# Norm steps and weight combinations moved in the last two matrix products of a fused attention, mixture and relu-squared kernel

## Chip, cores and metric

One core of one Trainium2 chip runs the kernel. The metric is the device time of one execution in microseconds (us); the median of three runs stands for a kernel. A profiled execution is one more run, with its own time.

## What is computed

Causal windowed attention with a linear bias, then a layer of eight experts of which each token uses one (top gate), then a second feed-forward block. The part that matters here is the last one:

```python
def _moe2_ref(x, w_in, w_out):      # x: 2304 x 512, w_in: 512 x 2048, w_out: 2048 x 512
    h = x @ w_in
    r = np.maximum(h, 0.0)
    g = r * r
    return (g @ w_out).astype(np.float32)
```

## The kernel before

Only the last part, `moe2`, is touched; it starts at about 417 us of the trace. It works in 9 groups G of 256 tokens. Numbers are kept as two 16-bit parts, hi (a cast on ScalarE, ACT) and lo (a subtraction on VectorE, DVE), and each product is three matmuls: hi hi, hi lo, lo hi. Both products use Winograd's form of Strassen's scheme: seven block products in place of eight, with sums of blocks made beforehand (S1 to S4 of one operand, T1 to T4 of the other).

**First product** (`wide1(G, m)`, one call for each half m of the hidden columns; "narrow pass" in what follows): seven block products (`product`, line 1165), 24 matmuls of 128 columns each, written to PSUM banks a and b (and c while G is below SG = 3). ACT copies three results out (`keep`, line 1178), DVE joins the others (line 1179). `square` then makes relu and square (lines 1194, 1195) and the hi and lo halves (`halves`, lines 1185, 1186) that the second product needs. From G = 3 on it also makes blocks S1 to S4 of the activations; for these GpSimd (POOL) makes two differences (lines 1198, 1201). c00, the block A11, is halved in `square(0)`; everything else in `square(1)`, where S4 and S3 (`z` and `p1`) are halved together as `pair(1)`.

**Second product**: `wide2(G, m)` for G below 3 (matmuls of 512 columns, lines 1334 to 1336) and `seven(G, part)` from G = 3 on: seven products for each half m, 12 matmuls of 256 columns each (line 1292). Part 0 has A11 B11, A12 B21, A22 T4 for m = 0 and then for m = 1. Part 1 has S2 T2, S3 T3, S1 T1, S4 B22, each for both halves. Results are added up on DVE (lines 1279, 1307), scaled in `put` on ACT (line 1316) and stored by an indirect DMA that POOL issues (line 1318).

**Order on TensorE** for a group G: part 0 of the second product of G, `wide1(G+1, 0)`, part 1 of G, `wide1(G+1, 1)`.

**Norm.** `norm(G+2)` is a generator whose steps are called between products: Abs on ACT (line 1108); eight small matmuls with a column of ones (line 1113) and a diagonal from them on DVE (line 1122); two small matmuls with the diagonal (line 1127) and a multiplication of the inputs by the result (line 1128); combinations T1 to T4 of the inputs (lines 1134 to 1137; POOL when G is above 3, else DVE) and their hi casts and lo subtractions (lines 1144, 1145). All these use the scratch buffer `dec`.

**Weight combinations.** `mix(k)`, k = 0 to 7, combines blocks of w_out into T1 to T4 on POOL (lines 1261 to 1266) in a scratch buffer (`SCRATCH` says which; otherwise `dec`) and writes hi and lo halves (ACT, line 1268; DVE, line 1269). The table `mixes` in `moe2` says after which stage each is written; 6 and 7 are written after `wide2(2, 1)` and before `wide1(3, 1)`, as seven(3, 0) is the first to use them.

The order in which instructions are written is not the order on an engine: a planner orders each engine's instructions ahead of time, by its own estimate of when operands are ready, and lets a later one go ahead of one that it thinks is waiting. On the chip each engine then takes them in that fixed order. `tc.issue_after(x)` keeps the instructions of a block behind instruction x on x's engine.

Of the kernel before, what the change touches and what calls it, by code (L numbers as in the profile page):

```python
# [23 lines left out]
P = 128  # L24
# [25 lines left out]
SCRATCH = {0: 0, 1: 1, 2: 1, 7: 4}  # L50
# [41 lines left out]
class K:  # L92
# [1007 lines left out]
    def norm(self, G, ab, tt):  # L1100
# [30 lines left out]
        Q = nc.gpsimd if G > SG else V  # L1131
# [5 lines left out]
        Q.tensor_tensor(t4, b[:, 1, 0], t2, op=ALU.subtract)  # L1137
        hi, lo = self.xts[G] = [self.part(G % 2 * 7168 + 3584 * a, 14 * P, F16).rearrange("p (c n) -> p c n", c=14)
# [30 lines left out]
    def wide1(self, G, m, between=lambda k: None):  # L1169
# [7 lines left out]
        pair = lambda k: self.part(22528 + 4096 * k, 8 * P).rearrange("p (o j n) -> p o j n", o=2, j=4)  # L1177
# [6 lines left out]
        def halves(hi, lo, src):  # L1184
            nc.scalar.copy(hi, src)  # L1185
            V.tensor_tensor(lo, src, hi, op=ALU.subtract)  # L1186

        def square(i):
# [15 lines left out]
            halves(*both(g[1]), pair(0))  # L1204
            V.tensor_tensor(z, c[:, :, 1, 0], u, op=ALU.subtract)
            halves(*both(g[2]), pair(1))
# [18 lines left out]
    def left(self, G, m):  # L1225

        g = self.gts[G, m]
        t = g[0].rearrange("p a (j t n) -> p a j t n", j=4, t=2)
        s = [x.rearrange("p a (o j n) -> p a o j n", o=2, j=4) for x in g[1:]]
        return {"A12": t[:, :, :, 0], "A22": t[:, :, :, 1], "S2": s[0][:, :, 0], "S1": s[0][:, :, 1],  # L1230
                "S4": s[1][:, :, 0], "S3": s[1][:, :, 1], "A11": s[2][:, :, 0]}
# [7 lines left out]
    def mix(self, k):  # L1239


        nc, Q, V = self.nc, self.nc.gpsimd, self.nc.vector
# [24 lines left out]
        for o in range(2):  # L1267
            nc.scalar.copy(y[o][:, :, 0], x[o])
            V.tensor_tensor(y[o][:, :, 1], x[o], y[o][:, :, 0], op=ALU.subtract)

    def seven(self, G, part, then):
# [7 lines left out]
        add = lambda dst, n, x: V.tensor_tensor(dst, ps[n], x, op=ALU.add)  # L1279
        if part == 0:  # L1280
            ps = self.py = [self.psum(t, [P, GW]) for t in "cdc"]
            names = (("A11", "B11"), ("A12", "B21"), ("A22", "T4"))
            order = [(n, m) for m in range(2) for n in range(3)]
        else:
            ps = [self.psum(t, [P, GW]) for t in "dcdd"]
            names = (("S2", "T2"), ("S3", "T3"), ("S1", "T1"), ("S4", "B22"))
            order = [(n, m) for n in range(4) for m in range(2)]
        for k, (n, m) in enumerate(order):
# [5 lines left out]
            if m == 1 and part == 0:  # L1294
                if n == 0:
                    nc.scalar.copy(b, ps[0])
# [17 lines left out]
    def put(self, G, i, o, src):  # L1314
        nc = self.nc
        nc.scalar.activation(o, src, AF.Copy, scale=self.fac[G][:, 1, i:i + 1])  # L1316
# [26 lines left out]
    def moe2(self):  # L1343
        NG = NT // GT
# [14 lines left out]
        mixes = {(0, 0): (0,), (0, 1): (1,), (0, 2): (2,), (1, 0): (3,), (1, 1): (4,), (2, 0): (5,), (SG, -1): (6, 7)}  # L1359

        def mix(G, k):
            for n in mixes.get((G, k), ()):
                self.mix(n)

        for G in range(NG):
            more, far = G + 1 < NG, G + 2 < NG
            if G < SG:
# [7 lines left out]
            if far:  # L1375
                nrm[G + 2] = self.norm(G + 2, None, None)
                next(nrm[G + 2])

            def then(k):
                if far and k in ((0, 2, 3) if G < SG else (0, 3, 5)):  # L1380
                    next(nrm[G + 2])
# [6 lines left out]
            if G + 1 == SG:  # L1388
                self.narrow = True
                mix(SG, -1)  # L1390
            if more:
                self.wide1(G + 1, 1)
# [60 lines left out]
```

## Time and profile before

| | before |
|---|---|
| median of 3 runs | 788.22 us (786.91 to 791.21) |
| profiled execution | 794.23 us, of which the span from first to last instruction 792.7 us |
| PE (TensorE matmuls) busy | 726.5 us, 92% |
| PEld (weight loads, beside PE) busy | 611.9 us, 77% |
| DVE busy | 592.9 us, 75% |
| ACT busy | 440.6 us, 56% |
| POOL busy | 236.4 us, 30% |
| mean granted TensorE clock | 0.969 |

Busy time is a share of the span of one profiled execution. A timeline row gives start, duration, engine, line, operation, tiles (written <- read), shapes and count; in brackets stands how long the engine had been idle before it and what ended that wait. Matmuls overlap, so a row of 24 matmuls shows about 0.15 us more than the step from its start to the next row's. The clock is a fraction of full speed; there are two levels, 1.2 and 2.4 GHz, so a value between them is a mean over the stretch.

### The profile page before, as it was taken

The page shows a single profiled execution, that of the slowest core. Times are in us where ns is not written, and L with a number is a line of the kernel's source. Part 1 is how long each engine was busy: PE and PEld are TensorE (multiplying, and loading weights), DVE is VectorE, ACT ScalarE, POOL GpSimd, SP SyncE. Part 2 cuts the span into 40 slices and gives each one's busy share as a digit, 9 for nine tenths or more (in the row PEclk, how much of TensorE's full clock was granted, in tenths as well). Part 3 has the DMA queues.
Part 4 walks back from the last instruction along what each step waited for, and adds up shares of the span by engine and source line. Part 5 has one row for each costly group of instructions (what it writes and reads, how often), then busy time and mean ns, then how long its engine had stood idle before and what let it go on. Part 6 is the DMA issues. An engine that isn't in the chain of part 4 may idle for free.

```text
span 792.7 us, 19608 instructions
## 1 busy us (share of the span) xinstructions
PE 726.5 (92%) x7979; PEld 611.9 (77%) x7979; DVE 592.9 (75%) x1414; ACT 440.6 (56%) x730; POOL 236.4 (30%) x275
## 2 busy tenths in 40 slices
PE   6989999997979899997997999998798989899995
PEld 6889899787746567786896777775697979898994
DVE  5888888754679998877897777767776767677661
ACT  5878898643456565656433343344556465655550
POOL 4673421424623020000003742406413141414120
PEclk9999999899899999999899999999899999999998
DMA  9894215756698685486414000000000000000000
GB/s 347 292 393 101 66 55 152 222 148 160 228 309 304 235 264 180 132 278 197 133 31 135 1 28 2 28 2 27 1 2 28 2 28 2 28 2 28 2 28 27
DMA packets 35656, 91.71 MB, mean 116 GB/s; under 512 B 5209, under 2 KB 13547, under 8 KB 35547
## 3 DMA queue, kind: packets, MB, share of 16 engines
q1 hardware_dynamic: 29803, 75.77, 29.6%
q0 software_dynamic: 5760, 14.65, 5.5%
q8 instruction: 64, 1.05, 0.6%
q14 instruction: 29, 0.24, 0.1%
HBM read 77.54 MB, written 13.04 MB: 114 GB/s over the span
## 4 chain that ended last, share of the span: by engine, by line
PE 45%; DVE 17%; issue 11%; DMA 10%; ACT 9%; POOL 6%; SPq 1%; POOLq 0%; DVEq 0%; ACTq 0%
PE ps_d L1292 6%; PE ps_a L1165 6%; PE ps_b L1165 5%; PE ps_a L308 5%; DMA rw<-in_w_dram 4%; DVE wr L768 3%; PE ps_b L331 3%; PE ps_c L363 3%; PE ps_c L1292 3%; PE ps_c L1165 2%; PE ps_d L1335 2%; PE ps_d L1336 2%; PE ps_d L1334 2%; DMA rw<-in_wi_dram 2%; ACT wr L767 2%
## 5 line engine op out<-in xcount | busy, mean ns | idle before, releaser
L1165 PEld LDWEIGHTS <-wi 128*128 128x128 f16 x3024 | 175.6, 99 | 19.5 <-issue 17.7
L1292 PEld LDWEIGHTS <-wr 128*128 128x128 f16 x1008 | 97.2, 98 | 20.7 <-DVE wr L1186 6.9
L1165 PE MATMUL ps_b<-work,wi 128*128 128x128 f16 x1272 | 82.0, 223 | 12.5 <-ACT work L1178 11.1
L1185 ACT CAST wr<-work 128x1024 f16<-128x1024 f32 (+1 forms) x60 | 57.6, 960 | 54.1 <-DVE work L1191 34.0
L848 PE MATMUL ps_c<-work,wr 128*128 128x352 f16 (+5 forms) x256 | 75.6, 298 | 11.2 <-DVE work L797 10.0
L1165 PE MATMUL ps_a<-work,wi 128*128 128x128 f16 x1344 | 85.8, 221 | 0.0
L847 PE MATMUL ps_c<-work,wr 128*128 128x352 f16 (+5 forms) x256 | 75.6, 298 | 6.0 <-ACT yT L850 3.1
L1186 DVE TENSOR_TENSOR wr<-work,wr 128x1024 f16<-128x1024 f32 (+1 forms) x60 | 73.0, 1219 | 9.6 <-ACT wr L1185 8.8
L849 PE MATMUL ps_c<-work,wr 128*128 128x352 f16 (+5 forms) x256 | 75.6, 298 | 0.0
L308 PE MATMUL ps_a<-yT,wr 128*128 128x192 f32 (+2 forms) x288 | 65.9, 350 | 5.7 <-DMA wr<-in_q_dram 5.0
L320 ACT ACTIVATE pb<-pb,nm 128x192 f32<-128x192 f32 (+2 forms) x144 | 56.3, 433 | 12.5 <-DVE nm L313 11.7
L767 ACT ACTIVATE wr<-rw 128x1024 f16<-128x1024 f32 x40 | 42.0, 1056 | 21.4 <-DMA rw<-in_w_dram 20.5
L768 DVE SCALAR_TENSOR_TENSOR wr<-rw,wr 128x1024 f16<-128x1024 f32 x40 | 48.7, 1221 | 5.4 <-ACT wr L767 5.3
L313 DVE CUSTOM_DVE_ANT_0 pb<-ps_a,bias 128x192 f32<-128x192 f32 (+2 forms) x144 | 44.2, 326 | 10.4 <-PE ps_a L308 8.3
L308 PEld LDWEIGHTS ps_a<-yT,wr 128*128 128x128 f32 x288 | 46.2, 203 | 6.9 <-DMA yT<-in_k_dram 5.5
L1261 POOL TENSOR_TENSOR yT<-wr 128x512 f32<-128x512 f16 x6 | 10.0, 1665 | 137.4 <-ACTq L1062 122.5
L1198 POOL TENSOR_TENSOR work<-work 128x512 f32<-128x512 f32 x12 | 15.3, 1274 | 106.5 <-ACT work L1195 106.5
L849 PEld LDWEIGHTS <-wr 128*128 128x128 f16 x288 | 29.5, 102 | 21.6 <-issue 13.8
L331 PE MATMUL ps_b<-cst,pb 128*128 128x128 f32 x256 | 45.3, 289 | 0.5 <-ACT pts L335 0.4
L1318 POOL DMA_INDIRECT out_dram<-o,oid x18 | 19.9, 1106 | 79.0 <-ACT o L1316 59.6
L1194 ACT ACTIVATE work<-work 128x1024 f32<-128x1024 f32 x24 | 25.4, 1056 | 29.9 <-DVE work L1179 29.9
L848 PEld LDWEIGHTS <-wr 128*128 128x128 f16 x288 | 29.5, 102 | 14.8 <-issue 7.0
(294 smaller groups left out, 1943.1 us busy)
## 6 DMA issues: line engine op xcount, KB each, us to landing
rw<-in_w_dram SPq DMA_DIRECT2D x40, 512.0 KB, 6.0
wi<-in_w_dram SPq DMA_DIRECT2D x20, 512.0 KB, 5.1
rw<-in_wo_dram SPq DMA_DIRECT2D x16, 512.0 KB, 4.4
rw<-in_wi_dram SPq DMA_DIRECT2D x32, 256.0 KB, 4.8
wr<-in_q_dram SPq DMA_DIRECT2D x14, 512.0 KB, 13.4
xd<-xhl POOLq DMA_DIRECT2D x16, 256.0 KB, 5.4
yT<-in_k_dram SPq DMA_DIRECT2D x7, 576.0 KB, 9.4
rw<-in_v_dram SPq DMA_DIRECT2D x12, 325.0 KB, 5.3
```

The source lines that it names most:

```text
L308: nc.tensor.matmul(ps[:, s, first:hi], q[g, u, hh // 4][:, hh % 4, s if u < 4 else 0, :], self.kt[g, hh // 2][:, hh % 2, key0:key0 + hi - ...
L320: self.last_exp = nc.scalar.activation(pb[:, s, first:hi], pb[:, s, first:hi], AF.Exp, bias=nm[:, s:s + 1], scale=-1.0)
L331: nc.tensor.transpose(pt[:, t, :, s, :], pb[:, s, t * P:(t + 1) * P], self.idf)
L767: self.nc.scalar.activation(t[:, 0], st, AF.Copy, scale=sc)
L768: self.nc.vector.scalar_tensor_tensor(t[:, 1], st, sc, t[:, 0], op0=ALU.mult, op1=ALU.subtract)
L847: nc.tensor.matmul(py, wh, hh, start=fc == 0, stop=False)
L848: nc.tensor.matmul(py, wh, hl, start=False, stop=False)
L849: self.last_mm = nc.tensor.matmul(py, wl, hh, start=False, stop=fc == 7)
L1165: self.nc.tensor.matmul(ps[:, j], w[:, kp, a, w0 * P:(w0 + 1) * P], v[:, 2 * x + kp], start=kp + b == 0, stop=kp == 1 and b == 2)
L1185: nc.scalar.copy(hi, src)
L1186: V.tensor_tensor(lo, src, hi, op=ALU.subtract)
L1292: nc.tensor.matmul(ps[n], x[:, v, j], y[j][:, w], start=m + i + j == 0, stop=m == 1 and i == 2 and j == 3)
```

## The change

- S3 T3 goes from part 1 of the second product to part 0. The halves of S3 (`p1`) are made in `square(0)` next to those of A11, in the same tile. Part 0 now has A11, A12, A22, S3 for m = 0 and A11, S3, A12, A22 for m = 1 (A11, A12, S3, A22 in group 3). The sums at the end of `seven` are put in another order, parts of the output are scaled earlier, and the last store has no scaling of its own.
- Norm steps from group 3 on are spread: Abs and the small matmuls in part 0, the multiplication and POOL's combinations in `wide1(G+1, 0)`, the hi casts in part 1, the lo subtractions in `wide1(G+1, 1)`. In every group each step's ACT and DVE instructions are kept behind the last halves, copy, store scaling or sum written before it (`end_act`, `end_dve`). The combinations of norm 4 are made on DVE instead of POOL.
- `mix` is cut in two: POOL's combination, and the casts and subtractions, which are kept behind `end_act` and `end_dve`. `MIXES` says when each half is written; combination 4 gets a scratch column of its own. The casts of 7 and 6 are written after `wide1(3, 1)`.

```diff
-SCRATCH = {0: 0, 1: 1, 2: 1, 7: 4}
+SCRATCH = {0: 0, 1: 1, 2: 1, 4: 3, 7: 4}
+MIXES = {(0, 4): (0,), (0, 0): (1,), (0, 1): (0,), (0, 2): (1,), (1, 4): (2, 3), (1, 1): (2, 3),
+         (2, 4): (4, 5), (2, 1): (4, 5), (2, 2): (7, 6), (2, 3): (7, 6)}
@@ norm
-        Q = nc.gpsimd if G > SG else V
+        late = G >= SG + 2
+        Q = nc.gpsimd if late else V
...
+        if late:
+            yield
...
-        for o, src in ((0, y[:, :, 0]), (4, y[:, 2:, 1]), (6, t)):
+        parts = ((0, y[:, :, 0]), (4, y[:, 2:, 1]), (6, t))
+        for o, src in parts:
             n = src.shape[1]
             nc.scalar.copy(hi[:, o:o + n], src)
+            if not late:
+                V.tensor_tensor(lo[:, o:o + n], src, hi[:, o:o + n], op=ALU.subtract)
+        yield
+        for o, src in parts if late else ():
+            n = src.shape[1]
             V.tensor_tensor(lo[:, o:o + n], src, hi[:, o:o + n], op=ALU.subtract)
         yield
@@ wide1
         def halves(hi, lo, src):
-            nc.scalar.copy(hi, src)
-            V.tensor_tensor(lo, src, hi, op=ALU.subtract)
+            self.end_act = nc.scalar.copy(hi, src)
+            self.end_dve = V.tensor_tensor(lo, src, hi, op=ALU.subtract)
...
                 halves(*(t[:, 0] for t in both(g[3])), c[:, :, 0, 0])
+                halves(*(t[:, 1] for t in both(g[3])), p1)
                 return
...
-            halves(*both(g[2]), pair(1))
+            halves(*(t[:, 0] for t in both(g[2])), z)
@@ mix
+        yield
+        with tc.issue_after(self.end_act.ins), tc.issue_after(self.end_dve.ins):
+            for o in range(2):
+                nc.scalar.copy(y[o][:, :, 0], x[o])
+                V.tensor_tensor(y[o][:, :, 1], x[o], y[o][:, :, 0], op=ALU.subtract)
@@ seven
-            names = (("A11", "B11"), ("A12", "B21"), ("A22", "T4"))
-            order = [(n, m) for m in range(2) for n in range(3)]
+            names = (("A11", "B11"), ("A12", "B21"), ("A22", "T4"), ("S3", "T3"))
+            order = [(n, 0) for n in range(4)] + [(n, 1) for n in ((0, 3, 1, 2) if G > SG else (0, 1, 3, 2))]
         else:
-            names = (("S2", "T2"), ("S3", "T3"), ("S1", "T1"), ("S4", "B22"))
-            order = [(n, m) for n in range(4) for m in range(2)]
+            names = (("S2", "T2"), ("S1", "T1"), ("S4", "B22"))
+            order = [(n, m) for n in range(3) for m in range(2)]
...
                 if n == 1:
-                    add(a, 1, b)
+                    self.end_dve = add(a, ps[1], b)
+                    scale(a)
             elif m == 1:
                 if n == 0:
-                    add(b, 0, b)
+                    add(b, ps[0], b)
+                    add(d, self.py[3], b)
+                    add(c, self.py[2], d)
                 elif n == 1:
-                    add(c, 1, b)
-                elif n == 2:
-                    add(d, 2, c)
-                    add(b, 2, b)
-                    V.tensor_tensor(c, self.py[2], c, op=ALU.add)
+                    add(b, ps[1], b)
+                    scale(b)
+                    add(d, ps[1], d)
                     self.put(G, 1, self.os[1], self.os[1])
                 else:
-                    add(b, 3, b)
-                    self.put(G, 0, self.os[0], self.os[0])
+                    V.scalar_tensor_tensor(b, ps[2], f[:, 0:1], b, op0=ALU.mult, op1=ALU.add)
+                    self.put(G, 0, self.os[0])
@@ moe2
+            def step():
+                with tc.issue_after(self.end_act.ins), tc.issue_after(self.end_dve.ins):
+                    next(nr)
+
+            at(G, 4)
             if G < SG:
                 self.wide2(G, 0)
             else:
-                self.seven(G, 0, lambda n: None)
-            mix(G, 0)
+                self.seven(G, 0, lambda k: step() if k in (5, 7) else None)
+            at(G, 0)
             if more:
-                self.wide1(G + 1, 0)
-            mix(G, 1)
...
+                self.wide1(G + 1, 0, lambda k: step() if G >= SG and k < 2 else at(G, 1) if k == 1 else None)
             if G < SG:
-                self.wide2(G, 1, then)
+                step()
+                self.wide2(G, 1, lambda k: step() if k != 1 else None)
...
-                self.seven(G, 1, then)
-            mix(G, 2)
...
+                self.seven(G, 1, lambda k: step() if k == 3 else None)
+            at(G, 2)
             if more:
-                self.wide1(G + 1, 1)
+                self.wide1(G + 1, 1, lambda k: step() if G >= SG and k == 0 else None)
+            at(G, 3)
```

## Rows read from the trace of the kernel before

**Rows 1.** Stretches: us; busy by engine (instructions); clock, DMA share, GB/s.
```profile
434.00:544.00 110.00, 109.85 (x1157) 75.86 (x1158) 83.20 (x122) 42.48 (x58) 43.10 (x38) 1.00 0.04 13
...
553.10:558.20 5.10, 5.02 (x48) 5.01 (x48) 4.01 (x2) 0.52 (x2) 5.07 (x6) 0.50 0.15 55
```

**Rows 2.** Waits of PE, 560 to 792 us: total us, times, longest.
```profile
PE ps_b L1165 <- ACT work L1178: 7.4, 5, 3.6
PE ps_d L1292 <- DVE wr L1186: 5.1, 5, 1.1
PE ps_d L1292 <- ACT wr L1185: 1.8, 3, 0.6
```

**Rows 3.** Chain that ended last: start, us, what (one product of each kind).
```profile
622.80 1.34 PE ps_a L1165 x24
624.14 1.31 PE ps_d L1292 x12
```

**Rows 4.** Timeline of PE, steady groups (columns as explained under the profile).
```profile
572.19 0.61 PE L1292 MATMUL ps_d<-rw,wr 128*128 128x256 f16 x4 [0.86 <-DVE wr L1186]
...
600.59 1.50 PE L1165 MATMUL ps_b<-work,wi 128*128 128x128 f16 x24 [0.95 <-ACT work L1178]
...
641.25 1.50 PE L1165 MATMUL ps_b<-work,wi 128*128 128x128 f16 x24 [0.96 <-ACT work L1178]
```

**Rows 5.** Timeline of ACT, one steady group.
```profile
597.77 1.05 ACT L1144 CAST work<-dec 128x1024 f16<-128x1024 f32 x1 [2.58 <-POOL dec L1137]
...
600.44 1.04 ACT L1108 ACTIVATE dec<-yT 128x1024 bf16<-128x1024 f32 x1
...
609.60 1.05 ACT L1185 CAST wr<-work 128x1024 f16<-128x1024 f32 x1
...
622.22 1.06 ACT L1194 ACTIVATE work<-work 128x1024 f32<-128x1024 f32 x1 [2.81 <-DVE work L1179]
```

**Rows 6.** Timeline of DVE, the same group.
```profile
595.15 2.00 DVE L1145 TENSOR_TENSOR work<-yT,work 128x512 f16<-128x512 f32 x2
...
598.85 1.23 DVE L1145 TENSOR_TENSOR work<-dec,work 128x1024 f16<-128x1024 f32 x1 [1.36 <-ACT work L1144]
...
607.56 1.22 DVE L1186 TENSOR_TENSOR wr<-work,wr 128x512 f16<-128x512 f32 x1 [0.88 <-ACT wr L1185]
```

**Rows 7.** Timeline of POOL, the same group.
```profile
606.96 1.27 POOL L1198 TENSOR_TENSOR work<-work 128x512 f32<-128x512 f32 x1 [2.50 <-ACT work L1195]
```

**Rows 8.** Timeline of PE, second narrow pass of group 3.
```profile
553.18 2.72 PE L1165 MATMUL ps_b<-work,wi 128*128 128x128 f16 x24 [3.63 <-ACT work L1178]
...
562.07 2.64 PE L1165 MATMUL ps_b<-work,wi 128*128 128x128 f16 x24 [3.60 <-ACT work L1178]
```

**Rows 9.** Timeline of ACT, the last halves before that pass and a cast in it.
```profile
540.03 1.04 ACT L1185 CAST wr<-work 128x1024 f16<-128x1024 f32 x1
...
552.02 0.62 ACT L1268 CAST rw<-yT 128x512 f16<-128x512 f32 x1 [3.05 <-POOL yT L1264]
```

**Rows 10.** Timeline of POOL, first and last of 12 operations of combinations 6 and 7.
```profile
547.26 2.26 POOL L1261 TENSOR_TENSOR yT<-rw 128x512 f32<-128x512 f16 x2
...
559.81 1.05 POOL L1266 TENSOR_TENSOR dec<-dec 128x256 f32<-128x256 f32 x1
```

**Rows 11.** Timeline of PE, the small norm matmuls in group 2.
```profile
535.63 0.34 PE L1113 MATMUL ps_c<-onesb,dec 128*128 128x1 bf16 x8
```

**Rows 12.** Timeline of PE, entry: a small norm matmul inside a product.
```profile
429.44 0.26 PE L1127 MATMUL ps_b<-sd,onesb 128*128 128x128 bf16 x1 [4.02 <-DVE sd L1122]
...
429.82 2.23 PE L1165 MATMUL ps_c<-work,wi 128*128 128x128 f16 x19
```

**Rows 13.** Timeline of DVE, entry: halves of combination 0.
```profile
422.34 0.69 DVE L1269 TENSOR_TENSOR xm<-yT,xm 128x512 f16<-128x512 f32 x1 [2.09 <-ACT xm L1268]
424.30 0.69 DVE L1269 TENSOR_TENSOR xm<-yT,xm 128x512 f16<-128x512 f32 x1 [1.27 <-ACT xm L1268]
```

**Rows 14.** Timeline of ACT, the scaling before the first of the last two stores.
```profile
782.18 0.72 ACT L1316 ACTIVATE o<-o,fac 128x512 f32<-128x512 f32 x1 [9.32 <-DVE o L1307]
```

More of the change, by code (lines that the diff above doesn't have):

```diff
@@ L1176, in wide1 @@
         u, p5, z, p1 = (self.part(22528 + 2048 * k, 4 * P).rearrange("p (j n) -> p j n", j=4) for k in range(4))
-        pair = lambda k: self.part(22528 + 4096 * k, 8 * P).rearrange("p (o j n) -> p o j n", o=2, j=4)
         keep = lambda dst, ps: nc.scalar.activation(dst, ps, AF.Copy, scale=RSC)
@@ L1203, in square @@
             V.tensor_tensor(u, p5, c[:, :, 0, 0], op=ALU.subtract)
-            halves(*both(g[1]), pair(0))
+            halves(*both(g[1]), self.part(22528, 8 * P).rearrange("p (o j n) -> p o j n", o=2, j=4))
             V.tensor_tensor(z, c[:, :, 1, 0], u, op=ALU.subtract)
-            halves(*both(g[2]), pair(1))
+            halves(*(t[:, 0] for t in both(g[2])), z)
         keep(p1, mul(A11, B11))
@@ L1278, in seven @@
         a, b, c, d = (o[:, h * GW:(h + 1) * GW] for o in self.os for h in range(2))
-        add = lambda dst, n, x: V.tensor_tensor(dst, ps[n], x, op=ALU.add)
+        f = self.fac[G][:, 1]
+        add = lambda dst, p, x: V.tensor_tensor(dst, p, x, op=ALU.add)
+        scale = lambda x: nc.scalar.activation(x, x, AF.Copy, scale=f[:, 0:1])
         if part == 0:
-            ps = self.py = [self.psum(t, [P, GW]) for t in "cdc"]
-            names = (("A11", "B11"), ("A12", "B21"), ("A22", "T4"))
-            order = [(n, m) for m in range(2) for n in range(3)]
-        else:
-            ps = [self.psum(t, [P, GW]) for t in "dcdd"]
-            names = (("S2", "T2"), ("S3", "T3"), ("S1", "T1"), ("S4", "B22"))
-            order = [(n, m) for n in range(4) for m in range(2)]
+            ps = self.py = [self.psum(t, [P, GW]) for t in "cdcd"]
+            names = (("A11", "B11"), ("A12", "B21"), ("A22", "T4"), ("S3", "T3"))
+            order = [(n, 0) for n in range(4)] + [(n, 1) for n in ((0, 3, 1, 2) if G > SG else (0, 1, 3, 2))]
+        else:
+            ps = [self.psum(t, [P, GW]) for t in "cdc"]
+            names = (("S2", "T2"), ("S1", "T1"), ("S4", "B22"))
+            order = [(n, m) for n in range(3) for m in range(2)]
         for k, (n, m) in enumerate(order):
@@ L1343, in moe2 @@
     def moe2(self):
-        NG = NT // GT
+        NG, tc = NT // GT, self.tc
         self.overflow()
@@ L1358, in moe2, with at @@
         self.fetch_out()
[L1359 to L1363, printed above, removed]
+        def at(*key):
+            for n in MIXES.get(key, ()):
+                if n in mixing:
+                    for _ in mixing.pop(n):
+                        pass
+                else:
+                    mixing[n] = self.mix(n)
+                    next(mixing[n])
+        mixing = {}
         for G in range(NG):
             more, far = G + 1 < NG, G + 2 < NG
+            nr = nrm[G + 2] = self.norm(G + 2, None, None) if far else iter([None] * 9)
+            def step():
+                with tc.issue_after(self.end_act.ins), tc.issue_after(self.end_dve.ins):
+                    next(nr)
+            at(G, 4)
             if G < SG:
@@ L1369, in moe2 @@
             else:
-                self.seven(G, 0, lambda n: None)
-            mix(G, 0)
+                self.seven(G, 0, lambda k: step() if k in (5, 7) else None)
+            at(G, 0)
             if more:
-                self.wide1(G + 1, 0)
-            mix(G, 1)
[L1375 to L1381, printed above, removed]
+                self.wide1(G + 1, 0, lambda k: step() if G >= SG and k < 2 else at(G, 1) if k == 1 else None)
             if G < SG:
-                self.wide2(G, 1, then)
-            else:
-                self.seven(G, 1, then)
-            mix(G, 2)
-            if G + 1 == SG:
-                self.narrow = True
-                mix(SG, -1)
+                step()
+                self.wide2(G, 1, lambda k: step() if k != 1 else None)
+                if G + 1 == SG:
+                    self.narrow = True
+            else:
+                self.seven(G, 1, lambda k: step() if k == 3 else None)
+            at(G, 2)
             if more:
-                self.wide1(G + 1, 1)
+                self.wide1(G + 1, 1, lambda k: step() if G >= SG and k == 0 else None)
+            at(G, 3)
 @with_exitstack
```

14 lines of the change are left out of this document (6 added, 8 removed).

## The prediction

> **What bounds the kernel now.** I read the busy table first: TensorE is busy 92% of the span, so only its gaps can be won, and only the last part of the kernel (from about 417 us on, the second expert block) is touched. Next, the stretches of that part: from 434 to 544 us PE is busy 109.85 of 110 us at clock 1.00 [rows 1], so there nothing can be gained and something can be lost. The gaps lie in three places. Which wait ends last at each is told by PE's waits and by the timelines.
>
> *The steady groups* (the seven-product form, 564 to 784 us). PE waits 7.4 us in 5 pieces for the copies of line 1178 (one of them the 3.6 of the transition, so 3.8 in 4 pieces here) and 5.1 + 1.8 us in 8 pieces for the halves of lines 1186 and 1185 [rows 2]. A group takes 641.25 - 600.59 = 40.66 us [rows 4]; its work is 14 products of 1.34 and 14 of 1.31 [rows 3], plus some 0.3 for the two small norm products, 37.4. So 3.2 us of a group are lost for 2.65 of listed waiting: a wait costs about 1.2 times what is listed. The first wait (0.95 and 0.96, the fifth product of the second narrow pass) is ACT: its queue stands 2.58 us at a norm cast that POOL's combinations feed, and then does the next norm's Abs between two copies that free PE's banks [rows 5]. The second is the A12 product of half 1, which wants that half's cast and then its subtraction on DVE (0.86 in the first group [rows 4]; some 1.7 in two pieces in each of the next).
>
> *The transition* (545 to 565 us). Fifth and seventh product wait 3.63 and 3.60 us [rows 8] for copies that stand on ACT behind casts of combined w_out, which wait for POOL [rows 9]. Three products around them take about 2.7 instead of 1.34, and the granted clock is 0.50, that is 1.2 GHz, from 553.1 to 558.2 [rows 1]; the rows show it fall after PE had been idle for 3.6 us. Together 7.2 + 3 x 1.3 = 11.1 us.
>
> *The entry* (425 to 434 us). PE waits 4.02 us inside a product, at a small norm matmul, for a diagonal that DVE makes late, and the 19 matmuls after it take 2.23 us where at full clock they would take about 1.1 [rows 12]. DVE was late because it stood 2.09 and 1.27 us at halves of combination 0 and did them (0.69 each) ahead of that norm step [rows 13].
>
> **The change, part by part.** *S3 T3 into part 0.* The twelve-matmul products stay 14 a group. In part 0 the A12 product of half 1 now has two more products in front of it (S3 of both halves): 2 x 1.31 = 2.6 us later, against a wait of about 1.7. Its own operands come a little later, since the cast and subtraction of 1024 become two of 512: ACT 2 x 0.62 - 1.05 = +0.2 [rows 5, 9], DVE 2 x 0.69 - 1.23 = +0.15 [rows 6, 13], with DVE busy 75% and ACT 56% of the span. The extra cast must wait for a POOL subtraction of 1.27 [rows 7]; if ACT holds its queue there, everything behind it slips up to 1.3 us. The cover is enough: in the first half pass, which has no ACT block ahead of it, the relu starts at 622.22, 1.9 us before the pass ends (624.14, [rows 3, 5]); with the block gone the second pass should look like that, 1.8 us earlier than now.
>
> *Norm steps spread and pinned.* Abs can no longer jump into the second narrow pass; POOL's combinations are made a pass earlier, so the cast does not stand in the queue. That takes the 0.95 away, 4 times. What comes late next is DVE: the norm's low halves (2.00 + 1.23 us [rows 6]) now sit in the second narrow pass ahead of the joins that feed the relu, and eat up to 3 of the 1.8 + 2.6 us of slack. Steady groups, then: (3.8 + 6.0) us listed (6.9 less the 0.86 of the first group, counted below) x 1.2 = 11.8, less 0 to 6 of new waiting; I take 2: **9.8 us** (6 to 11.8).
>
> On DVE against POOL, a row first: a 128x512 subtraction takes 1.22 us at 607.56, while POOL works from 606.96 to 608.23, and 0.69 at 422.34, after POOL's piece has ended [rows 6, 7, 13]. The Trainium skill ("SBUF — State Buffer", section "SBUF: two separate sides") says that the two share a port pair as an exclusive lock and that the loser "fully blocks". This trace agrees (1.22 against 0.69), and by that rule the new 512 piece, if it meets the second POOL operation, costs 1.22 rather than 0.69, about 0.5 more twice a group, all of it inside the slack above.
>
> *Transition.* The casts of combinations 6 and 7 go behind the second pass of group 3, so copies are free and that pass should run through: the fifth product would start at 549.55, the pass end at 553.6. But POOL is no faster. Its two combinations run from 547.26 to 560.9 now [rows 10]. The norm's four combinations leave POOL for DVE, which starts it earlier; the norm's Abs is pinned behind the last halves (540.03 + 1.05 [rows 9]), which starts it later. I take an end at 562. Behind that, in order: POOL's two subtractions of this pass (2 x 1.27), a DVE step (0.7), two casts (1.05, 0.62), then the pinned casts (0.62 each, the third is the one S3 needs) and a subtraction (0.69): about 569. PE reaches S3 of half 1 at 553.6 + 6 x 1.31 = 561.4. So the 7.2 us of waiting come back as one wait of about 7 on PE, six products further on, and a slow-clock stretch after it (about 2 us). Part 0 then ends near 573.5; before, the same eight products would have been done at 562.07 + 2.64 + 8 x 1.31 + 0.9 = 576. Gain **3 us**; ends 0 (POOL two or three us later) and 12 (all waiting of 11.1 and 0.9 hidden).
>
> *Entry.* Combination 0's casts are pinned behind the halves of the pass in which they now disturb: DVE gets back 2.09 + 1.27 + 2 x 0.69 = 4.7 us ahead of the diagonal. Wait and slow clock cost 4.0 + 1.4; I take **4 us** (0 to 5.4; the place of the small matmul may move with it).
>
> *Pins in the saturated stretch.* Abs of groups 2 to 4 may now start only behind the last halves of the pass before. In group 2 the small norm matmul stood at 535.63 [rows 11], the last cast at 540.03 to 541.08 [rows 9]. The order on PE is planned, so wide matmuls should go ahead of it, but the plan misses by a microsecond or more (the entry's 4.02 is such a miss). I charge **1.5 us** for three groups (0 to 6).
>
> *Tail.* The first of the two stores waited for a 0.72 us scaling at 782.18 [rows 14], behind three DVE steps; now two precede it, and the second store is fed by DVE alone; since the second store waits for the first, what the first gains counts: **0.35 us** (0 to 0.7). MIXES for combinations 1 to 5 and the order of adds: nothing, under the full PE of 434 to 544; if that cover fails it shows in the pin term.
>
> **Sum.** 9.8 + 3 + 4 - 1.5 + 0.35 = 15.65 us. The profiled execution took 794.23 (span 792.7), so it would take 778.6. The median of the runs is 788.22, 6 lower; the same microseconds off it give **772.5**.
>
> **Rivals.** (1) *The transition is fully hidden*: POOL ends by 556 or so, PE waits 1 us; 12 in place of 3: 763.5. For: one combination has a scratch column of its own; against: 12 us of POOL work still start near 548. (2) *The A12 wait only moves*: norm subtractions on DVE and the cast that waits for POOL eat the slack, and 0.9 us stay at each half of a group: steady gain 5: 777. For: DVE is the busiest engine behind PE. Against: 2.6 us of new cover. (3) *Slower: PE in order, at the pinned norm.* If the small matmul stays at its written place, PE waits in group 2 from 535.6 until Abs is done, 541.1 + 1.05: 6.5 us, and about 2.6 for the slow clock after it; groups 0 and 1 likewise, at worst the same, 27 us in all, less 15.65 + 1.5: some 10 slower, 798. It decides from about 6 us a group on; with 3 a group the gain is halved. Against: planned order puts small matmuls between others already (the entry's stands inside a product). (4) *The pins do nothing new* (these casts and steps were late in the queue anyway): only the S3 move pays, 6 x 1.2 us and the tail's 0.35: 780.5.
>
> **How the numbers follow.** Forecast 0.52 (769 to 776), rival 1 0.13, rival 2 0.15, rival 4 0.08, rival 3 0.07, and 0.05 for a mixture of pins and transition that comes out at no change. The range to hold 8 of 10 leaves out the fastest half of rival 1 and rival 3 with the no-change cases: 763 to 783. About 0.5% (4 us) is what a measurement of this kernel can tell from no change. Faster by more than that (below 784.3): 0.87; within: 0.07; slower: 0.06.
>
> **What would show it.** In the profile after: steady period 37.5 to 38 instead of 40.66; no PE wait for line 1178's copies after 570 us; no 4 us gap at 425; between 545 and 554 seven products without a gap, then one gap of several microseconds in part 0 of group 3 ending on a cast or subtraction of a combination. Wrong if PE shows gaps at the small norm matmuls between 434 and 544 (rival 3), if A12 still waits each group (rival 2), or if the gap of group 3 is under 2 us (rival 1).

## The result, and the profile after

The changed kernel takes 780.93 us (median of 16 runs, 776.7 to 785.21) against 788.17 for the kernel before (16 runs, 783.43 to 791.92). The ratio is 0.9912, with a 95% interval of 0.9887 to 0.9937: some 7 us faster, less than half of the 15.65 forecast. The profiled execution took 782.72 us. Its page begins:

```profile
span 780.8 us, 19641 instructions
PE 718.3 (92%) x7979; PEld 601.6 (77%) x7979; DVE 592.3 (76%) x1430; ACT 443.3 (57%) x748; POOL 236.2 (30%) x271
```

Totals of single executions can't be compared to a microsecond here. The touched part begins behind a branch (the `tc.If` that the profiles name as line 1062 or 1064), and the first narrow product behind it, which waits for that branch and for nothing of the change, begins at 418.19 us in the profile of before, at 415.15 in that of after, and between 410.27 and 416.72 in the experiments. So I compare from that product on, in five stages, each bounded by the start of a pass on PE. *Entry* is from that product to the next wide product (the second half of group 0), *stretch* from there to the second narrow pass of group 3, *transition* from there to the second narrow pass of group 4, *steady* the four groups up to the second narrow pass of group 8, *tail* the rest of the span. Times are us, the stages from one profiled execution each:

| kernel | entry | stretch | transition | steady | tail | sum | median, or the one run |
|---|---|---|---|---|---|---|---|
| before | 15.73 | 110.11 | 50.09 | 161.35 | 37.23 | 374.51 | 788.17 |
| **after** | 12.30 | 113.89 | 47.06 | 155.73 | 36.67 | 365.65 | 780.93 |
| e1_norm_unpinned | 12.30 | 112.09 | 46.83 | 155.10 | 36.66 | 362.98 | 781.57 |
| e2_timed | 12.29 | 112.57 | 45.98 | 149.33 | 36.64 | 356.81 | 770.85 |
| e3_hi_before_store | 12.29 | 115.39 | 47.05 | 154.69 | 36.66 | 366.08 | 780.32 |
| e4_l1_in_pass | 12.28 | 115.40 | 47.50 | 162.62 | 36.66 | 374.46 | 788.49 |
| e5_s3_move_alone | 15.76 | 112.14 | 49.35 | 166.39 | 36.67 | 380.31 | 795.18 |
| e6_combinations_alone | 12.29 | 110.08 | 45.43 | 161.33 | 37.18 | 366.31 | 780.02 |
| e7_s3_cast_behind_a12 | 12.08 | 112.79 | 43.99 | 152.84 | 36.63 | 358.33 | 770.23 |
| e8_and_early_norm_unpinned | 12.30 | 110.77 | 44.88 | 152.77 | 36.61 | 357.33 | 772.60 |
| e9_both | 12.16 | 110.78 | 44.82 | 149.62 | 36.65 | 354.03 | 767.17 |
| e10_s3_back | 12.29 | 112.57 | 43.64 | 153.39 | 37.17 | 359.06 | 772.58 |

After against before gains 3.4 at the entry, loses 3.8 in the stretch, gains 3.0 in the transition, 5.6 in the steady groups and 0.6 in the tail: 8.9 together. (The other 3.0 us of the two spans' difference lie before the branch.) How far one profile can be trusted is shown by e2's kernel, which was profiled twice: the sum is 355.18 in one and 356.81 in the other, and 1.4 of the 1.6 us lie in the transition (44.55 and 45.98); the other stages agree within 0.3. So a difference of a microsecond between two rows shows nothing in the transition or the sum.

PE's waits from 560 to 780 us show what is new; these lines answer to [rows 2] (total us, times, longest):

```profile
PE ps_d L1307 <- ACT wr L1195: 4.2, 1, 4.2
PE ps_b L1176 <- ACT work L1188: 2.9, 4, 0.7
PE ps_a L1115 <- ACT dec L1110: 2.0, 3, 0.7
PE ps_d L1307 <- ACT wr L1281: 1.3, 1, 1.3
PE ps_d L1307 <- DVE wr L1196: 0.2, 1, 0.2
```

The waits of A12 that stood in every steady group are gone. What is left there are two waits: in each group that of the fifth product of the second narrow pass, at the copies (now line 1188), as before but 0.73 us instead of 0.95; and, new, in the three of them that have norm steps, that of the small norm matmuls (now 1115), at Abs. PE's timeline has each of them, with the entry and the end of the stretch, in answer to [rows 4, 8, 11, 12]:

```profile
424.37 0.22 PE L1129 MATMUL ps_b<-sd,onesb 128*128 128x128 bf16 x1 [1.98 <-DVE sd L1124]
...
537.84 0.34 PE L1115 MATMUL ps_c<-onesb,dec 128*128 128x1 bf16 x8 [2.50 <-ACT dec L1110]
...
561.60 1.89 PE L1307 MATMUL ps_d<-rw,wr 128*128 128x256 f16 x8 [4.17 <-ACT wr L1195]
...
594.65 1.50 PE L1176 MATMUL ps_b<-work,wi 128*128 128x128 f16 x24 [0.73 <-ACT work L1188]
...
610.03 0.34 PE L1115 MATMUL ps_a<-onesb,dec 128*128 128x1 bf16 x8 [0.65 <-ACT dec L1110]
```

All but the first end on ACT. ACT's own timeline says what it did before, in the transition and in one steady group (compare [rows 5, 9]):

```profile
552.90 0.62 ACT L1195 CAST wr<-work 128x512 f16<-128x512 f32 x1
557.81 0.62 ACT L1195 CAST wr<-work 128x512 f16<-128x512 f32 x1 [4.29 <-POOL work L1208]
558.33 1.05 ACT L1204 ACTIVATE work<-work 128x1024 f32<-128x1024 f32 x1
...
591.23 0.51 ACT L1294 ACTIVATE o<-o,fac 128x256 f32<-128x256 f32 x1 [1.78 <-DVE o L1293]
...
594.02 0.58 ACT L1188 ACTIVATE work<-ps_b 128x512 f32<-128x512 f32 x1
...
601.53 0.62 ACT L1195 CAST wr<-work 128x512 f16<-128x512 f32 x1 [0.73 <-POOL work L1208]
602.05 1.05 ACT L1204 ACTIVATE work<-work 128x1024 f32<-128x1024 f32 x1
...
608.04 0.62 ACT L1195 CAST wr<-work 128x512 f16<-128x512 f32 x1 [0.69 <-DVE work L1216]
608.57 0.36 ACT L1311 COPY o<-ps_c 128x256 f32<-128x256 f32 x1
608.83 1.06 ACT L1110 ACTIVATE dec<-yT 128x1024 bf16<-128x1024 f32 x1
```

The cast at 601.53 is S3's. ACT stands 0.73 us in front of it until POOL has made the difference it casts, and relu and square of the second half of the pass (lines 1204, 1205), whose input DVE had finished at 599.95, come behind it; with them A12's cast, the copy at 608.57 and the Abs at 608.83 for which PE then waits. What is late at the end of one pass is late in the next: in the one before, the scaling at 591.23 waits for DVE's sums, these stand behind the subtraction that goes with the last cast, and the copy at 594.02, for which the fifth product waits, comes behind scalings and norm casts. The planner had put S3's cast ahead of that relu. In the transition the same place costs 4.29 us, since POOL has the two combinations in front of that difference (compare [rows 10]):

```profile
543.84 2.27 POOL L1272 TENSOR_TENSOR yT<-rw 128x512 f32<-128x512 f16 x2
...
555.83 0.73 POOL L1277 TENSOR_TENSOR dec<-dec 128x256 f32<-128x256 f32 x1
556.51 1.26 POOL L1208 TENSOR_TENSOR work<-work 128x512 f32<-128x512 f32 x1
```

Stretches of after (us; busy by engine; clock last but two) answer to [rows 1]: PE is no longer full in the stretch, runs the second narrow pass of group 3 without a gap, and has a mean clock of 0.53, near the lower of the two levels, from 560 us on, in and behind the 4.17 us wait:

```profile
427.45:541.34 113.89, 110.46 (x1158) 75.67 (x1158) 90.48 (x129) 44.94 (x62) 47.35 (x37) 1.00 0.04 13
541.34:550.72 9.38, 9.38 (x169) 9.38 (x168) 8.45 (x12) 3.73 (x7) 7.75 (x7) 1.00 0.08 30
560.00:571.00 11.00, 7.81 (x42) 5.14 (x43) 6.91 (x10) 6.99 (x11) 1.26 (x1) 0.53 0.01 1
```

### The profile page after: what moved, and what is told of

Read it like the earlier page. It is cut to its first block, busy times and chain, and to the rows that moved or that the text cites. A ratio compares the mean times of both kernels' runs of the same rounds, so it can differ in the third digit from the quotient of the medians.

```text
span 780.8 us, 19641 instructions
## 1 busy us (share of the span) xinstructions
PE 718.3 (92%) x7979; PEld 601.6 (77%) x7979; DVE 592.3 (76%) x1430; ACT 443.3 (57%) x748; POOL 236.2 (30%) x271
## 5 line engine op out<-in xcount | busy, mean ns | idle before, releaser
L1176 PEld LDWEIGHTS <-wi 128*128 128x128 f16 x3024 | 170.5, 98 | 8.8 <-issue 7.3
L1307 PEld LDWEIGHTS <-wr 128*128 128x128 f16 x1008 | 99.2, 99 | 20.1 <-ACT wr L1195 4.4
L1195 ACT CAST wr<-work 128x1024 f16<-128x1024 f32 (+1 forms) x72 | 59.9, 832 | 77.6 <-DVE work L1201 44.5
L1176 PE MATMUL ps_b<-work,wi 128*128 128x128 f16 x1368 | 85.5, 219 | 4.4 <-ACT work L1188 2.9
L1196 DVE TENSOR_TENSOR wr<-work,wr 128x1024 f16<-128x1024 f32 (+1 forms) x72 | 74.7, 1051 | 15.3 <-ACT wr L1195 13.1
L1176 PE MATMUL ps_a<-work,wi 128*128 128x128 f16 x1248 | 78.2, 219 | 0.0
L310 PE MATMUL ps_a<-yT,wr 128*128 128x192 f32 (+2 forms) x288 | 64.2, 342 | 6.8 <-DMA wr<-in_q_dram 5.2
L322 ACT ACTIVATE pb<-pb,nm 128x192 f32<-128x192 f32 (+2 forms) x144 | 56.1, 432 | 12.6 <-DVE nm L315 11.8
L851 PEld LDWEIGHTS <-wr 128*128 128x128 f16 x288 | 29.4, 102 | 21.5 <-issue 14.4
L333 PE MATMUL ps_b<-cst,pb 128*128 128x128 f32 x256 | 43.7, 281 | 0.5 <-ACT pts L337 0.4
L850 PEld LDWEIGHTS <-wr 128*128 128x128 f16 x288 | 29.4, 102 | 17.6 <-issue 10.2
L778 POOL DMA_INDIRECT xg<-xd,idx x21 | 24.3, 1158 | 51.6 <-PE ps_d L786 40.8
```

The lines of the kernel that those rows point to most:

```text
L310: nc.tensor.matmul(ps[:, s, first:hi], q[g, u, hh // 4][:, hh % 4, s if u < 4 else 0, :], self.kt[g, hh // 2][:, hh % 2, key0:key0 + hi - ...
L322: self.last_exp = nc.scalar.activation(pb[:, s, first:hi], pb[:, s, first:hi], AF.Exp, bias=nm[:, s:s + 1], scale=-1.0)
L333: nc.tensor.transpose(pt[:, t, :, s, :], pb[:, s, t * P:(t + 1) * P], self.idf)
L850: nc.tensor.matmul(py, wh, hl, start=False, stop=False)
L851: self.last_mm = nc.tensor.matmul(py, wl, hh, start=False, stop=fc == 7)
L1176: self.nc.tensor.matmul(ps[:, j], w[:, kp, a, w0 * P:(w0 + 1) * P], v[:, 2 * x + kp], start=kp + b == 0, stop=kp == 1 and b == 2)
```

## The experiments

The theory: S3's cast, where it stands on ACT, costs what its move should have brought. Its rivals: the pins of the norm; the place of single norm steps; or that the terms of the forecast were simply too large.

**The norm without its pins.** All of the change but `issue_after` around the norm's steps.

```diff
             def step():
-                with tc.issue_after(self.end_act.ins), tc.issue_after(self.end_dve.ins):
-                    next(nr)
+                next(nr)
```

> The changed kernel with the norm steps written where the change puts them, but not kept behind the last halves, copies and sums (the weight combinations stay pinned). Theory: the pins of the norm steps make Abs late and with it the small norm matmuls. Then the waits of 0.4, 0.5 and 2.5 us at these matmuls between 434 and 544 us go, and the saturated stretch (first wide matmul of the second half of group 0 to the second narrow pass of group 3) falls from 113.9 to about 110.3 us; in the steady groups the 0.65 us wait goes but Abs or the hi casts jump elsewhere, so the period of 39.2 us changes by less than 1 us either way. Rival: the steps are late because of where they are written; then all these waits stay as they are.

781.57 us in one run. PE's waits from 417 to 780 us, largest first:

```profile
PE ps_c L1307 <- DVE o L1293: 4.0, 4, 1.0
PE ps_d L1307 <- ACT wr L1195: 2.9, 1, 2.9
PE ps_a L1129 <- DVE fac L1165: 2.1, 1, 2.1
...
PE ps_b L1176 <- ACT work L1188: 1.6, 4, 0.7
```

No wait for Abs is left, but stretch, transition and steady groups gain 1.8, 0.2 and 0.6 us only; in the steady groups DVE takes over, with 1.02 us a group at the bank of the S4 product, and 0.3 to 0.7 of the copies' wait stays. The pins have a price, in the stretch above all, but they are not what halved the gain.

**S3's cast behind the square.** The pins stay; S3's halves are written in `square(1)`, behind the square of the second half.

```diff
@@ wide1, square(0)
-                halves(*(t[:, 1] for t in both(g[3])), p1)
                 return
@@ square(1)
-            nc.scalar.activation(ci, ci, AF.Square, scale=0.5)
+            squared = nc.scalar.activation(ci, ci, AF.Square, scale=0.5)
             halves(...A12...)
+            with tc.issue_after(squared.ins):
+                halves(*(t[:, 1] for t in both(g[3])), p1)
```

> The changed kernel with the cast of S3 moved behind the square of the second half of a pass on ACT, so that ACT does not stand in its queue for POOL's difference. Theory: the 4.2 us wait of A12 in part 0 of group 3 is that queue (ACT stood 4.3 us there for POOL); then A12 runs through, and what is left is one wait at S3 and its weights of some 2 to 4 us, so the 29.7 us from the start of the second narrow pass of group 3 to the end of part 0 fall by 1 to 3 us. Rival: POOL's end sets it whatever ACT does; then S3 waits as much as A12 did and the 29.7 us stay within 0.7. Steady period unchanged (39.2) by both, since A12 does not wait there.

772.53 us in one run, and in a second series of 5 runs, timed beside the kernel before, 770.85 (768.17 to 773.18), a ratio of 0.9779 (0.9747 to 0.9811).

> The same kernel as e2, timed: one edit on the changed kernel, S3's cast behind the square. By the theory 9 to 11 us below the changed kernel, ratio to the kernel before near 0.979; by the rival (POOL's end or the pins set the time) 0.987 or above.

One moved cast brings 10 us by the medians, 8.8 in the stages of this profile. The steady period falls from 39.18 to 37.41 us, which is what 14 + 14 products and the norm's small ones take, and PE waits nowhere behind group 3. Its waits from 535 to 755 us (second series):

```profile
PE ps_d L1308 <- ACT wr L1195: 2.4, 1, 2.4
PE ps_d L1308 <- ACT wr L1282: 1.3, 1, 1.3
PE ps_d L1308 <- DVE wr L1196: 0.4, 1, 0.4
```

On ACT the relu now runs while POOL subtracts, and S3's cast (one of the two at 596.33) needs no waiting; both 0.73 and 0.65 are gone, though only the one cast was moved. My expectation for the first run was wrong here: I had put the whole gain into group 3 and the steady period at an unchanged 39.2, since A12 did not wait there.

```profile
593.75 0.62 ACT L1195 CAST wr<-work 128x512 f16<-128x512 f32 x1
594.28 1.05 ACT L1204 ACTIVATE work<-work 128x1024 f32<-128x1024 f32 x1
595.36 1.06 ACT L1205 ACTIVATE work<-work 128x1024 f32<-128x1024 f32 x1
596.33 1.55 ACT L1195 CAST wr<-work 128x512 f16<-128x512 f32 x2
```

**Single norm steps elsewhere.** Two tries at the two waits from the norm's side. e3 has the hi casts one product earlier in part 1 (`k == 3` becomes `k == 2`), so that they are out of the copies' way:

> The changed kernel with the norm's hi casts written one product earlier in part 1, so ahead of the two scalings of the store on ACT. Theory: the 0.73 us wait of the fifth product of the second narrow pass in each steady group is ACT's queue of scaling, store scaling and hi casts (until 594.0 us in the first one); with the hi casts first it empties about 0.9 us earlier, the wait goes, and the period falls from 39.2 to 38.3 or 38.4. Rival: the wait comes from the sums on DVE that the scalings need; then it stays near 0.7 and the period at 39.2.

780.32 us in one run. The 0.73 is gone, the 0.65 stays, A12 waits again, and the period of a group with norm steps is 39.0 to 39.4, not the 38.3 that I had given. Two of PE's waits from 417 to 780 us:

```profile
PE ps_a L1115 <- ACT dec L1110: 2.4, 4, 0.7
PE ps_d L1307 <- DVE wr L1196: 2.4, 4, 1.0
```

e4 has the small matmuls, and so Abs's deadline, in the next narrow pass (part 0: a step at 5 alone; `wide1(G+1, 0)`: a step at each of three products):

> The changed kernel with the eight small norm matmuls, the two with the diagonal and POOL's combinations each written one place later from group 3 on (the small ones inside the first narrow pass instead of right behind part 0). Theory: the 0.65 us wait at the small matmuls in each steady group (four of them) is the pinned Abs, which ends 0.2 us before them; three products later it is long done, so the wait goes and the period falls from 39.2 to about 38.4. Rival: what is moved collides later, at the diagonal or at the hi casts, and a wait of that size stands there instead; period 39.2 or more.

788.49 us in one run: in the steady groups the wait for Abs is gone, all norm steps come later, and the fifth product waits 2.47 us four times. The period is about that of before (40.5, once 41.8).

```profile
PE ps_b L1176 <- ACT work L1188: 9.9, 4, 2.5
```

As long as ACT is late in the group, a wait taken away at one place comes back at another.

**The parts alone.** e5 is the kernel before with S3's move and the new sums (`wide1`'s halves and `seven` of after), nothing of norm or combinations:

> The kernel before with the S3 product in part 0, its halves made with those of A11, and the new order of sums and scalings; norm steps and weight combinations as before. Theory: this part alone takes the A12 wait (1.7 us listed) out of each steady group but puts an ACT queue that stands for POOL into each pass, and leaves the 0.95 us wait of the copies; period between 39 and 40 us (before 40.7, the changed kernel 39.2); the transition (10.9 us lost) and the 4.0 us wait at 425 to 430 stay. Rival: S3 halves eat the slack and A12 goes on waiting; period 40.5 or more. Time 780 to 787 by the first, 788 or more by the second, before being 788.

795.18 us in one run: slower than before, which my theory had not allowed for. PE's waits from 417 to 780 us, then ACT's timeline in one group:

```profile
PE ps_b L1165 <- ACT work L1177: 18.8, 6, 4.4
```

```profile
584.14 0.62 ACT L1184 CAST wr<-work 128x512 f16<-128x512 f32 x1 [0.73 <-POOL work L1197]
...
597.37 1.04 ACT L1144 CAST work<-dec 128x1024 f16<-128x1024 f32 x1 [1.56 <-POOL dec L1137]
598.32 0.59 ACT L1177 ACTIVATE work<-ps_b 128x512 f32<-128x512 f32 x1
```

With the norm where it was, ACT stands three times for POOL in a group, 0.73 us at each cast of S3 and 1.56 at the norm cast, and PE's wait for the copies grows from 0.95 to 2.90. A12's wait is gone but for 0.79 us in two groups. The move costs 5.0 us in the steady groups and 2.0 in the stretch, and brings 0.7 and 0.6 in transition and tail.

e6 is the kernel before with the combinations of w_out cut, pinned and moved, and nothing else:

> The kernel before with only the weight combinations cut in two, their casts kept behind the queue, and the scratch column of combination 4. Theory: this part owns the entry and the second narrow pass of group 3: the 4.0 us wait near 426 falls to about 2, the pass of group 3 runs through in 9.4 us (20.5 before), and part 0 then waits some 6 to 8 us for S3-free products A12 and A22 and the casts of combinations 6 and 7, so the transition gains 2 to 5 us; the saturated stretch stays at 110 us, since the norm steps are not pinned; steady period 40.7 as before. Rival: the pins of the casts also cost in the saturated stretch; then it grows by 1 us or more.

780.02 us in one run: the entry's 3.4 us whole, 4.7 in the transition, and nothing lost in the stretch (110.08). This part alone gains 8.2 of the 8.9 us; norm and S3 together add 0.7, less than two profiles of one kernel differ by. Its steady groups are those of before (161.33).

e10 is the changed kernel with S3 in part 1 again, and the steps of part 0 at products 3 and 5:

> The changed kernel with the S3 product put back into part 1 (its halves made with S4's, the sums and scalings as before); norm steps spread and pinned, and weight combinations, as changed. Theory: without the cast that stands for POOL the small norm matmuls and the copies are on time, but A12 wants its halves 2.6 us earlier, so a wait of 0 to 1 us may stand there; period 37.5 to 38.5, below the 39.2 of the changed kernel, so that the S3 move as written costs rather than gains. Rival: the S3 move is what brings the period from 40.7 to 39.2; then the period is 40 or more here.

> The changed kernel with S3 in part 1 again (all else as changed), now timed beside the kernel before. Theory: the S3 move as it was made costs more on ACT than it covers on PE; one profiled execution without it took 359.1 us from the first narrow product after the branch to the end, against 365.7 with it and 374.5 before, so it should stand some 12 to 15 us below the kernel before: 773 to 778, a ratio of 0.980 to 0.986. Rival: that execution was a quick one and the S3 move costs nothing that can be measured: a ratio near that of the change, 0.99, about 781.

775.91 us in one run, then 772.58 (771.55 to 777.14, 6 runs), a ratio of 0.9803 (0.9772 to 0.9833). The intervals of this and of the change (0.9887 to 0.9937) are apart: **S3's move, as it was made, costs some 8 us** (the new sums, which go with it, included). In the stages of the two profiles (e10_s3_back against after) it is 6.6: 1.3 in the stretch, 3.4 in the transition and 2.3 in the steady groups, against 0.5 gained in the tail. The period is 38.67, just above what I had given for it, since the small norm matmuls, which I had thought would be on time, wait 0.81 us in three groups: part 0 is two products shorter here, and the pinned Abs is late for it even without S3's cast. All waiting of PE from 566 us on:

```profile
PE ps_a L1115 <- ACT dec L1110: 2.4, 3, 0.8
```

**A better place for the cast.** e7 puts S3's halves behind A12's cast instead of behind the square (`issue_after(self.end_act.ins)` after A12's halves):

> As e2, but the cast of S3 is kept behind the cast of A12 and A22 (one place further back). Theory: in group 3 ACT still stood 2.2 us for POOL ahead of the A12 cast, which held A12 for 2.4 us; now A12 runs through and S3 waits for the end of POOL's combinations and the pinned casts, some 3 to 4 us in one piece; the 27.2 us of second narrow pass and part 0 of group 3 become 25.5 to 27, the period stays at 37.4. Rival: S3 becomes the late operand in the steady groups as well, where it stands ahead of A12; then a wait appears there and the period grows to 38 or more.

770.23 us in one run. The transition takes 43.99 against the 45.98 and 44.55 of e2's two profiles, too little from the second to call it better; the steady groups are worse (38.27 a group against 37.41), as S3 itself now waits 0.46 for its subtraction, which was the rival. e8 takes e7 and leaves the norm's steps unpinned for groups below 3:

```diff
             def step():
+                if G < SG:
+                    next(nr)
+                    return
```

> As e7, and the norm steps of the first three groups are not pinned (from group 3 on they are). Theory: the waits of 0.4, 0.5 and 1.2 us at the small norm matmuls between 434 and 544 us come from Abs behind the last halves; without the pins the first two go, the third becomes a wait for the diagonal of at most 2 us as in e1, and the stretch falls from 112.6 to between 110.5 and 112 us. Rival: Abs ahead of the halves makes the next product late instead; the stretch stays at 112.5.

The stretch falls from 112.79 to 110.77, and the sum by half of that, as the transition is 0.9 longer in these two profiles. The time, 772.60 us in one run, is not below that of e7. e9 takes e8, with S3's cast behind A12's cast in group 3 and behind the square in the groups after:

```diff
+            with tc.issue_after(self.end_act.ins if G == SG else squared.ins):
+                halves(*(t[:, 1] for t in both(g[3])), p1)
```

> The changed kernel with three edits put together: S3's cast behind the square (behind A12's cast in group 3 only), and the norm steps of the first three groups not pinned. If the standing of ACT's queue for POOL and the early pins are what ate the gain, the touched part (first narrow product after the branch to the end) falls from 365.7 us in the changed kernel to 352 to 355, the steady period is 37.4, and the time is 11 to 14 us below the changed kernel, 17 to 20 below the kernel before (ratio to before near 0.976). Rival: the look at e2 was a lucky run; then the ratio to before stays at 0.985 or above.

767.17 us (766.05 to 769.52, 5 runs), a ratio of 0.9735 (0.9706 to 0.9764): faster than both kernels, and 21 us below the one before where I had given 17 to 20. What PE still waits for from 425 to 755 us are two products of group 3's part 0 and, ahead of them, a norm matmul at the end of the stretch:

```profile
PE ps_d L1308 <- ACT wr L1282: 2.8, 1, 2.8
PE ps_d L1308 <- DVE wr L1196: 2.6, 1, 2.6
PE ps_a L1129 <- DVE fac L1165: 0.8, 1, 0.8
```

## Why the prediction was right and wrong

The time lies in the range of 763 to 783 but outside the forecast of 769 to 776: the gain is 7.2 us for 15.65. The stages of one profile each make it 8.9; what they have above the 7.2 is no more than two profiles of one kernel differ by. So I go by the stages, term by term.

**What bounds the kernel**: held. Every gain and loss above is a gap of PE or the slow clock behind one.

**Entry, 4 us**: 3.4. The diagonal came earlier, PE waited 1.98 instead of 4.02, and the 19 matmuls after it ran at full clock. e6 shows that the combinations did it; their cut, their pins and their new places were not tried one by one.

**Transition, 3 us**: 3.0, but by luck, since errors cancel. The pass ran without a gap, as forecast. POOL ended its combinations 15.2 us after the start of the pass (556.5 less 541.34), between the 18 that I had taken (562 less 544.03) and the 12 that rival 1 asked for. PE waited 5.8 us in part 0 instead of 7, but for the most part at A12 of half 1 (4.17); at S3 behind the pinned casts, where I had put all of it, it waited 1.35. A12 was late by the unpinned cast of S3 in the same pass, in front of which ACT stood 4.29 us. And the slow clock cost nearly 4 us, not 2: from the start of the pass to the end of part 0 are 29.7 us, of which 19.9 are the products at full clock (7 x 1.34 and 8 x 1.31). Without S3's move this stage gives 6.4 us (e10).

**Steady groups, 9.8 us (6 to 11.8)**: 5.6, the term that was mis-sized. The failing step is "if ACT holds its queue there, everything behind it slips up to 1.3 us. The cover is enough". I had seen the wait for POOL, and its bound of 1.3 us held (0.73, twice a group), but I held it only against the A12 product, where the 2.6 us of cover did suffice. Behind the same queue stand also the Abs, with the small norm matmuls waiting for it at the end of part 0, and through the sums, scalings and norm casts the copies of the next narrow pass; for these S3's move gives no cover. So "That takes the 0.95 away, 4 times" came out as 0.95 to 0.73, with a new 0.65 three times. The 0.65 takes both causes, the early cast and the pin of Abs: it is gone without the one (e2) and without the other (e1). The 2 us that I had set aside were laid to DVE.

I also credited the wrong part. A12's wait, 6.0 of the 9.8 us of listed waits that I meant to win, was to be cured by S3's cover. In e10 it is gone with S3 in its old place, so the cover was not needed: the norm's order alone gives 8.0 us in the steady groups, S3's move alone -5.0 (e5), both as made 5.6, both with S3's cast behind the square 12.0 (e2_timed), the upper end of my range.

**Pins in the stretch, -1.5 (0 to -6)**: -3.8. Rival 3's mechanism took place at a small scale: 0.42, 0.51 and 2.50 us at the small matmuls, not 6.5 a group, as the planner did move them back. The stages split it: 110.11 before; 110.78 with S3's cast late and the norm of these groups unpinned (e9); 112.57 with the pins (e2_timed); 113.89 with S3's cast in its early place too. So the pins cost about 1.8, that cast 1.3, the rest 0.7. (The 113.89 is the lower of two times that the same instructions took, see the last section; by the 115.4 of e3 and e4 the cast costs 2.8.)

**Tail, 0.35**: 0.56; it stands in every kernel that has the new sums (36.6 to 36.7) and in none without (37.2).

**The rivals.** Rival 4 gave 780.5, which is nearly the time, for the reverse of the reason: it let S3's move pay and the pins do nothing. Rival 2 gave 777 for an A12 wait that in truth went; its 5 us for the steady groups came nearest to the 5.6, and it did name the cast that waits for POOL. The rival that I lacked was a standing ACT whose price falls on other products than those that S3 covers.

**The Trainium skill's rule** on the shared port ("SBUF — State Buffer", section "SBUF: two separate sides") says that the one who comes second waits for the whole instruction of the other. The trace of after agrees that it waits, with 3.09 us for a subtraction of 1.23 [rows 6], but there it waited for two operations of POOL in a row (last section). No wait of PE in the steady groups of after ends on DVE. One reading of mine was wrong: at 422.34 POOL had not ended. Its next operation runs from 422.54 to 423.61 and takes 1.07 us where one takes 0.73 with DVE idle (last section), so by the durations it was POOL that waited there; the 0.69 at 424.30 [rows 13] has POOL idle beside it.

## What to carry to other kernels

When a step is moved on an engine that takes its instructions in a fixed order, look for whoever stands *behind* the new place, not only for the consumer that the move is meant to help: follow the queue to the end of the group and name each waiting product. An operand that a slower engine makes should be cast behind whatever is ready already; here one cast put one relu and square later made 10 us by the medians. And where a change has several parts, price each alone: here, by the stages, one part gained 8, one more 7, and the third cost 7 of it.

## What I had not expected of the hardware

The clock after a wait is not the same in two executions of the same instructions. The 2.50 us wait at the small matmuls in group 2 stands in after, in e3 and in e4, which agree up to there. In after the clock stays at 1.00, that is 2.4 GHz, behind it; in e3 it falls, to 0.50 or 1.2 GHz from 537 to 539 us, and the stretch takes 115.39 instead of 113.89 us (115.40 in e4). The stretches behind that wait, after first (its end, to 537.84, is in it), e3 second:

```profile
537.00:541.40 4.40, 3.56 (x26) 1.72 (x27) 3.72 (x12) 1.17 (x2) 1.07 (x1) 1.00 0.17 63
```

```profile
536.00:540.00 4.00, 4.00 (x14) 1.54 (x12) 3.65 (x10) 0.92 (x2) 0.00 (x0) 0.57 0.13 46
```

One execution can show both. In e4 the fifth product waits 2.46 or 2.47 us in four groups; behind the third of these waits alone the clock is 0.50, and that group takes 41.82 us instead of 40.47 (the third wait, then the stretches behind the second and the third):

```profile
676.55 2.72 PE L1176 MATMUL ps_b<-work,wi 128*128 128x128 f16 x24 [2.46 <-ACT work L1188]
```

```profile
636.09:638.50 2.41, 2.41 (x44) 2.41 (x44) 2.31 (x4) 0.92 (x2) 0.91 (x1) 1.00 0.11 36
676.55:679.00 2.45, 2.45 (x24) 2.45 (x24) 2.35 (x4) 0.92 (x2) 0.98 (x1) 0.50 0.11 35
```

So a wait of this length has two prices, some 1.4 us apart. What decides between them no run here shows. The forecast's factor of 1.2 on listed waits held no room for that.

And a subtraction of DVE and an addition of POOL, both on SBUF, can hold each other up, in either direction. In after's transition one subtraction on DVE takes 3.09 us where [rows 6] has 1.23 for the same shape:

```profile
544.13 3.09 DVE L1152 TENSOR_TENSOR work<-dec,work 128x1024 f16<-128x1024 f32 x1 [0.83 <-ACT work L1150]
```

```profile
546.07 1.74 POOL L1274 TENSOR_TENSOR yT<-yT 128x256 f32<-128x256 f32 x1
547.88 1.06 POOL L1275 TENSOR_TENSOR yT<-yT 128x256 f32<-128x256 f32 x1
```

It ends at 547.22, that is 1.1 us behind the end of POOL's first pair of operations (543.84 + 2.27), about the time it takes alone; POOL's next one, at 546.07, takes 1.74 us in turn, where one of that size takes 0.73 with DVE idle (the one at 555.83 above), and 1.06 beside DVE's next subtraction. So by their durations these took turns, and DVE had to let two of POOL's operations pass.
